# Loads of v on GpSimd's queue, new transfer times in the planner, copies of q by ScalarE or VectorE, and a tail matmul over 128 rows

## The chip, the core and the metric

The kernel runs on one core of a Trainium2 chip. The time is device microseconds of one execution. The kernel before was timed in 3 runs: median 733.4 us (730.46 to 735.7).

## What is computed

An attention layer with soft-capped scores, and behind it a feed-forward block without gating. Shapes: 4 batches, 12 heads, 448 positions, 64 values per head; 1792 tokens, model width 768, inner width 2048.

```python
def _attn_ref(q, k, v, cap):                       # 4, 12, 448, 64
    scores = 1.0 / np.sqrt(q.shape[-1]) * np.matmul(q, k.transpose(0, 1, 3, 2))
    scores = cap * np.tanh(scores / cap)
    scores = scores - np.max(scores, axis=-1, keepdims=True)
    attn = np.exp(scores)
    attn = attn / (np.sum(attn, axis=-1, keepdims=True) + 1e-09)
    return np.matmul(attn, v)

def _moe_ref(x, w_in, w_out):                      # 1792x768, 768x2048, 2048x768
    h = x @ w_in
    return (h - np.tanh(h)) @ w_out
```

The weights come as 64-bit floats and are turned into 32-bit ones on the core.

## The kernel before, in words

**Work.** Heads are taken in pairs (batch b, pair p; 24 pairs, 6 to a batch). For each pair q and k are loaded (`fetch_qk`), transposed by VectorE, and split into a high and a low part (`prep_pair`); v is loaded (`fetch_v`). Scores are matmuls over 448 columns on TensorE (line 689, one pass with the high part of q and one with the low part, so a block of scores is two matmuls), ScalarE makes tanh (line 699) and exp (line 757), and the product with v (PV) is accumulated on TensorE. The first 11 pairs (`F32_PAIRS`) make PV in plain 32-bit floats (`pv_f32`, line 825; 8 matmuls to a pair, each in two records of the trace). The other 13 pairs split v and exp into high and low parts (`pv`): per head 3 blocks of keys with three matmuls each (lines 852, 853, 854), and a tail block of 64 keys with two (lines 849 and 850). In the tail block the 64 keys stand twice on the 128 partitions, the high part of exp on one half and the low part on the other. Line 849 multiplies the low part of v with the high part of exp alone, so it takes 64 of the 128 rows.

**Feed-forward.** For each batch 16 blocks of inner width are worked through: `first` (lines 1159 to 1161) makes h, then tanh and a difference, and `second` (line 1212) accumulates the output. In batch 0's turn each block of weights is loaded (`fetch_raw`, lines 1000 and 1012, 1.5 MB a block), decoded by three passes of VectorE (lines 1042, 1049, 1056), split, and the decoded form is stored to memory by GpSimd's queue (line 986, tile fuk); later batches load it from there. The attention of batch b+1 is interleaved with the feed-forward of batch b.

**Order.** Nothing is ordered by hand. `Plan` collects all instructions with a cost, an engine, what they depend on, and the buffers they take, and then plays them through with these costs (`schedule`): each engine (TensorE, ScalarE, VectorE, SyncE's queue, GpSimd's queue) takes the instruction that can start first. A transfer costs its queue an issue time, and then stands in one line with all other transfers for `nbytes * slow / 360` ns. What comes out is a fixed order on each engine. So a changed cost reorders every engine.

**What the change touches.** `Build.dma` (line 441) holds the issue costs. `fetch_qk` and `fetch_v` issue on SyncE's queue (lines 473, 500, 502, 505). In `prep_pair`, the first 12 pairs need the high part of q on both halves of the partitions: for pair 0 of batch 0 and for the pairs of batch 1 ScalarE or VectorE copies it (`self.copy`, lines 422 and 424 in the trace), for the other 5 pairs of batch 0 a DMA of GpSimd's queue does (line 606). The buffers of v for the first 11 pairs are two (tag `v1`), so the load of pair i waits until PV of pair i-2 is done. The two buffers `vraw` serve the other pairs.

## Time and profile before

| | |
|---|---|
| median of 3 runs | 733.4 us |
| the profiled execution | 728.99 us, span 727.1 us |
| TensorE matmul busy | 700.3 us, 96% |
| ScalarE, VectorE busy | 530.4 us (73%), 508.0 us (70%) |
| GpSimd busy | 46.2 us (6%) |
| granted TensorE clock, mean | 0.994 of full speed |

The span is the time between the first and the last instruction of the profiled execution. PE is TensorE's matmul, DVE VectorE, ACT ScalarE, POOL GpSimd; SPq is SyncE's queue of DMAs. Matmuls are pipelined, so one record is longer than its share of the time: the distance from one start to the next is what a matmul takes. An idle time of an engine stands with what ended it.

### The profile page before, as it was taken

The numbers are of one execution on the slowest core, as the hardware profiler recorded it, in microseconds if no ns is written. First come the engines' busy times: TensorE is split into PE (matmuls) and PEld (weight loads), VectorE is DVE, ScalarE is ACT, GpSimd is POOL, SyncE is SP. The second block draws the span as 40 slices with busy tenths as digits, with TensorE's granted clock in tenths as the row PEclk, the third lists the DMA queues.
The fourth block names the chain that finished last, engine by engine and source line by source line (L and its number), as shares of the span: only waits on it lengthen the run. The fifth ranks groups of instructions, "written<-read, shape, count | busy, mean of one in ns | idle before, by whom it ended". The sixth has DMA issues, their size and how long they took to land.

```text
span 727.1 us, 10148 instructions
## 1 busy us (share of the span) xinstructions
PE 700.3 (96%) x3648; PEld 606.2 (83%) x3648; DVE 508.0 (70%) x775; ACT 530.4 (73%) x891; POOL 46.2 (6%) x93
## 2 busy tenths in 40 slices
PE   7989899999999999999999999999999999999996
PEld 5656687787788888889989897888989999999995
DVE  5889999997999986586678785786675333333331
ACT  7978957666677986677779898988896554545543
POOL 3110000000210110110110110110000000000000
PEclk9999999999999999999999999999999999999998
DMA  7999999999998593753765887777648656665523
GB/s 111 170 175 235 205 264 272 241 275 256 239 273 224 172 244 116 169 148 119 166 147 162 259 219 191 182 197 211 188 125 266 169 147 174 174 173 141 149 60 114
DMA packets 161823, 136.75 MB, mean 188 GB/s; under 512 B 116772, under 2 KB 146756, under 8 KB 161764
## 3 DMA queue, kind: packets, MB, share of 16 engines
q1 hardware_dynamic: 156676, 116.78, 66.7%
q0 software_dynamic: 5088, 19.24, 8.8%
q8 instruction: 31, 0.51, 0.3%
q14 instruction: 28, 0.23, 0.1%
HBM read 107.12 MB, written 18.09 MB: 172 GB/s over the span
## 4 chain that ended last, share of the span: by engine, by line
PE 54%; DVE 18%; DMA 14%; ACT 6%; issue 3%; SPq 3%; POOL 0%; DVEq 0%; ACTq 0%; POOLq 0%
PE facc L1212 18%; PE fh L1159 7%; PE fh L1161 7%; PE fh L1160 7%; DMA fw<-in_moe_w_in_dram 5%; PE fs L689 4%; DVE fu L1056 2%; DMA fkst<-fkst 2%; DVE fu L1049 2%; DMA fkst<-fkT 2%; DVE fwo L433 2%; PE fp L1212 2%; PE fs L1212 2%; PE fp L852 2%; DVE fu L1042 1%
## 5 line engine op out<-in xcount | busy, mean ns | idle before, releaser
L1212 PE MATMUL facc<-fwo,fgh 128*128 128x512 f32 (+1 forms) x768 | 171.4, 345 | 0.0
L1212 PEld LDWEIGHTS facc<-fwo,fgh 128*128 128x128 f32 x768 | 127.0, 188 | 20.1 <-issue 6.2
L1159 PE MATMUL fh<-fxh,fwi 128*128 128x384 f32 x384 | 135.3, 352 | 1.5 <-DVE fg L1174 1.5
L1161 PE MATMUL fh<-fxh,fwi 128*128 128x384 f32 x384 | 130.0, 339 | 0.0
L1160 PE MATMUL fh<-fxl,fwi 128*128 128x384 f32 x384 | 128.6, 335 | 0.0
L1212 PE MATMUL facc<-fwo,fgl 128*128 128x512 f32 (+1 forms) x384 | 98.6, 338 | 0.0
L433 DVE TENSOR_TENSOR fwi<-fu,fwi 128x768 fp32r<-128x768 f32 x66 | 62.9, 953 | 47.0 <-ACT fwi L422 46.6
L422 ACT CAST fwi<-fu 128x768 fp32r<-128x768 f32 x60 | 50.1, 835 | 44.0 <-PE fh L1161 29.7
L1159 PEld LDWEIGHTS fh<-fxh,fwi 128*128 128x128 f32 x384 | 72.1, 188 | 7.5 <-DVE fg L1174 2.9
L1160 PEld LDWEIGHTS fh<-fxl,fwi 128*128 128x128 f32 x384 | 72.2, 188 | 4.1 <-issue 2.6
L433 DVE TENSOR_TENSOR fwo<-fu,fwo 128x768 fp32r<-128x768 f32 x66 | 62.7, 950 | 15.7 <-ACT fwo L422 15.3
L1174 DVE TENSOR_TENSOR fg<-fh,fg 128x384 f32<-128x384 f32 x64 | 35.6, 556 | 53.5 <-ACT fg L1172 52.5
L1161 PEld LDWEIGHTS fh<-fxh,fwi 128*128 128x128 f32 x384 | 72.0, 187 | 0.0
L1212 PEld LDWEIGHTS facc<-fwo,fgl 128*128 128x128 f32 x384 | 58.8, 188 | 8.6
L699 ACT ACTIVATE fe<-fs 128x448 f32<-128x448 f32 x91 | 49.2, 541 | 18.9 <-PE fs L689 18.4
L689 PE MATMUL fs<-fqst,fkst 128*128 128x448 f32 x142 | 55.7, 412 | 3.9 <-ACT fe L699 2.0
L422 ACT CAST fwo<-fu 128x768 fp32r<-128x768 f32 x62 | 51.4, 829 | 8.8 <-PE facc L1212 8.3
L1172 ACT ACTIVATE fg<-fh 128x384 f32<-128x384 f32 x64 | 31.1, 485 | 34.4 <-PE fh L1161 34.3
L422 ACT CAST feh<-fe 128x896 fp32r<-128x896 f32 (+1 forms) x64 | 50.8, 793 | 0.8
L757 ACT ACTIVATE fe<-fe,absc 128x896 f32<-128x896 f32 (+1 forms) x52 | 49.6, 954 | 0.9
L433 DVE TENSOR_TENSOR fel<-fe,feh 128x896 fp32r<-128x896 f32 x39 | 42.2, 1081 | 10.4 <-ACT feh L422 10.3
L689 PE MATMUL fs<-fql,fkst 128*128 128x448 f32 x142 | 49.1, 366 | 0.0
(195 smaller groups left out, 1327.2 us busy)
## 6 DMA issues: line engine op xcount, KB each, us to landing
fu<-fuk SPq DMA_DIRECT2D x48, 768.0 KB
fw<-in_moe_w_in_dram SPq DMA_DIRECT2D x64, 384.0 KB
fw<-in_moe_w_out_dram SPq DMA_DIRECT2D x32, 768.0 KB
fuk<-fu POOLq DMA_DIRECT2D x16, 768.0 KB, 7.2
fqst<-fqh POOLq DMA_DIRECT2D x48, 112.0 KB, 5.5
fqraw<-in_q_dram SPq DMA_DIRECT2D x44, 112.0 KB
fkraw<-in_k_dram SPq DMA_DIRECT2D x44, 112.0 KB
out_dram<-fo SPq DMA_DIRECT2D x12, 384.0 KB
```

The lines of the kernel that those rows point to most:

```text
L422: self.nc.scalar.copy(out(), in_())
L433: lambda: self.nc.vector.tensor_sub(lo(), x(), hi().bitcast(F32)),
L689: nc.tensor.matmul(ps()[:, :S], self.keys(kst, h, c), q[:, h, :], start=n == 0, stop=n == passes - 1)
L699: S, lambda: nc.scalar.activation(dst(), ps()[:, :S], AF.Tanh), [o],
L757: lambda e=e, w=w: nc.scalar.activation(e()[:, :w, :], e()[:, :w, :], AF.Exp, scale=self.absc),
L852: nc.tensor.matmul(P()[:, :S], va, e, start=c == 0, stop=False)
L1159: nc.tensor.matmul(h()[:, :n], wh, ah, start=(d == 0), stop=False)
L1160: nc.tensor.matmul(h()[:, :n], wh, al, start=False, stop=False)
L1161: nc.tensor.matmul(h()[:, :n], wl, ah, start=False, stop=(d == ND - 1))
L1172: n, lambda: nc.scalar.activation(g()[:, :n], h()[:, :n], AF.Tanh), [prev], [g], [h], psum=True, key=k
L1174: o = self.dve(n, lambda: nc.vector.tensor_sub(g()[:, :n], h()[:, :n], g()[:, :n]), [o], [], [g, h], key=k + 600)
L1212: nc.tensor.matmul(banks[bk]()[:, c0 : c0 + ne], lhs()[:, ts], w()[:, k, e0 : e0 + ne], start=bk in firsts and bk not in begun, stop=stop ...
```

## The change

Five edits. The four loads of v of a pair are issued by GpSimd's queue in place of SyncE's. The copies of q in batch 0 are no DMAs any more: all are `self.copy`, and the planner chooses ScalarE or VectorE. The planner's costs change: issue of a DMA by SyncE 475 to 550 ns, by GpSimd 1016 to 600; the factor of q and k 2 to 2.3, of v 1 or 2 to 1.8, of the moves of k and q inside the chip 1 to 1.5. The tail's matmul with the low part of v takes all 128 rows, so the product of the two low parts is added, which the kernel before left out there. The new order follows from the costs.

```diff
     def dma(self, eng, nbytes, fn, deps=(), alloc=(), uses=(), slow=1, long=False, key=1e18):
-        c = (650.0 if long else 475.0) if eng == "SP" else 1016.0
+        c = (650.0 if long else 550.0) if eng == "SP" else 600.0
...
-                    self.dma("SP", np_ * S * 128, fn, [], [] if ops else [raw], [raw] if ops else [], slow=2)
+                    self.dma("SP", np_ * S * 128, fn, [], [] if ops else [raw], [raw] if ops else [], slow=2.3)
...
-                        nc.sync.dma_start(out=t[:, 0:3, :], in_=full.rearrange("(r c) d -> r c d", c=3))
+                        nc.gpsimd.dma_start(out=t[:, 0:3, :], in_=full.rearrange("(r c) d -> r c d", c=3))
                     elif f32:
-                        nc.sync.dma_start(out=t[TAIL * hp : TAIL * hp + TAIL, 3, :], in_=tail)
+                        nc.gpsimd.dma_start(out=t[TAIL * hp : TAIL * hp + TAIL, 3, :], in_=tail)
                     else:
-                        nc.sync.dma_start(out=t[:, 3, :], in_=tail.unsqueeze(0).to_broadcast([2, TAIL, D]))
+                        nc.gpsimd.dma_start(out=t[:, 3, :], in_=tail.unsqueeze(0).to_broadcast([2, TAIL, D]))
...
-                        "SP", (128 if part else FULL) * 256, fn, [], [] if ops else [vr],
-                        [vr] if ops else [], slow=1 + (f32 or part), long=f32 or part,
+                        "PL", (128 if part else FULL) * 256, fn, [], [] if ops else [vr],
+                        [vr] if ops else [], slow=1.8, long=True,
...
-                    [], [], [kst, T["k"]],
+                    [], [], [kst, T["k"]], slow=1.5,
...
-                if p == 0 or b:
-                    o3 = self.copy(
-                        S, lambda other=other, hp=hp: qst()[other, hp, :],
-                        lambda rows=rows, hp=hp: qst()[rows, hp, :].bitcast(F32), [o1], [], [qst],
-                    )
-                else:
-                    o3 = self.dma("PL", 64 * S * 4, dup, [o1], [], [qst])
+                o3 = self.copy(
+                    S, lambda other=other, hp=hp: qst()[other, hp, :],
+                    lambda rows=rows, hp=hp: qst()[rows, hp, :].bitcast(F32), [o1], [], [qst],
+                )
...
-                o3 = self.dma("PL", 64 * S * 4, dup, [o1], [] if i else [qst], [qh] + [qst] * (i > 0))
+                o3 = self.dma("PL", 64 * S * 4, dup, [o1], [] if i else [qst], [qh] + [qst] * (i > 0), slow=1.5)
...
                 if c == 3:
-                    nc.tensor.matmul(num, v2()[rows, c, hp, :], e[rows], start=False, stop=False)
+                    nc.tensor.matmul(num, v2()[:, c, hp, :], e, start=False, stop=False)
                     nc.tensor.matmul(P()[:, :S], va, e, start=False, stop=True)
```

How the order moves, at the places that the prediction speaks of. The first is SyncE's queue in batch 0, from the loads of k and q of pairs 2 and 3 on, before (fqraw and fkraw are q and k as loaded, fv1float the buffers of v of the first 11 pairs, fw a block of raw weights):

```order
L473 DMA fkraw_263<-in_k_dram 32x28x32 x4
L473 DMA fqraw_289<-in_q_dram 32x28x32 x4
L473 DMA fkraw_308<-in_k_dram 32x28x32 x2
L500 DMA fv1float_172<-in_v_dram 128x3x64 x2
L502 DMA fv1float_172<-in_v_dram 64x64 x2
L473 DMA fkraw_308<-in_k_dram 32x28x32 x2
L1000 DMA fw_50_356<-in_moe_w_in_dram 64x6x128 x2
L1012 DMA fw_50_356<-in_moe_w_out_dram 128x768
L473 DMA fqraw_382<-in_q_dram 32x28x32 x4
L473 DMA fkraw_408<-in_k_dram 32x28x32
L500 DMA fv1float_239<-in_v_dram 128x3x64 x2
L502 DMA fv1float_239<-in_v_dram 64x64 x2
```

And the same place in the changed kernel:

```order
L473 DMA fkraw_239<-in_k_dram 32x28x32 x4
L473 DMA fqraw_264<-in_q_dram 32x28x32 x4
L473 DMA fkraw_300<-in_k_dram 32x28x32 x4
L993 DMA fw_42_328<-in_moe_w_in_dram 64x6x128 x2
L1005 DMA fw_42_328<-in_moe_w_out_dram 128x768
L993 DMA fw_47_353<-in_moe_w_in_dram 64x6x128 x2
L1005 DMA fw_47_353<-in_moe_w_out_dram 128x768
L473 DMA fqraw_394<-in_q_dram 32x28x32 x4
```

The loads of v are gone from the queue, so 33 DMAs stand ahead of the first weights in place of 45, and the second block of weights follows the first at once.

The second place is GpSimd's queue in the changed kernel, from the load of v of pair 2 on (L979 is line 986 of before, the store of a decoded block of weights):

```order
L500 DMA fv1float_131<-in_v_dram 128x3x64 x2
L502 DMA fv1float_131<-in_v_dram 64x64 x2
L500 DMA fv1float_166<-in_v_dram 128x3x64 x2
L502 DMA fv1float_166<-in_v_dram 64x64 x2
L500 DMA fv1float_131<-in_v_dram 128x3x64 x2
L502 DMA fv1float_131<-in_v_dram 64x64 x2
L979 DMA fuk_87<-fu_486 128x1536
L500 DMA fv1float_166<-in_v_dram 128x3x64 x2
L502 DMA fv1float_166<-in_v_dram 64x64 x2
L500 DMA fv1float_131<-in_v_dram 128x3x64 x2
L502 DMA fv1float_131<-in_v_dram 64x64 x2
L979 DMA fuk_88<-fu_631 128x1536
```

The rows are the loads of pairs 2, 3, 4, a store, those of pairs 5 and 6, and a store. The loads of pairs 7, 8, 9 and 10 stand behind stores in the same way, and the loads of two late pairs (tile fvraw) stand just ahead of this place. In the kernel before this queue held the ten DMAs of q and the stores.

The third place is VectorE in batch 0, around the first decode in the changed kernel (fu is the block being decoded, fsumT_512 the sums of pair 2, fkst_103 and fql_107 the split k and q of pair 4):

```order
L909 TENSOR_TENSOR fx_475<-fnum_389,frb_458 128x384
L915 TENSOR_TENSOR fxt_116<-fnum_389,frb_458 128x64
L530 STREAM_TRANSPOSE fkT_482<-fkraw_300 128x448
L1035 TENSOR_SCALAR fu_486<-fw_42_328 128x1536
L424 CAST fkst_103<-fkT_482 64x448
L424 CAST fxh_495<-fx_475 128x384
L556 TENSOR_TENSOR fkst_103<-fkT_482,fkst_103 64x448
L424 CAST fkst_103<-fkT_482 64x448
L1042 SCALAR_TENSOR_TENSOR fu_486<-fw_42_328,fu_486 128x1536
L875 STREAM_TRANSPOSE fsumT_512<-fp_477 64x448
```

The first pass of the first decode (L1035, before L1042) stands ahead of the split of pair 4's k and of the sums of pair 2. Before, it stood behind the sums of pair 2 and the split of pair 4's k.

Over the whole program the copies of q on ScalarE go from 13 to 19 and on VectorE from 1 to 5; the count of matmuls stays the same.

## Rows read from the trace of the kernel before

**Rows 1.** Part 1 of the page: busy time, share of the span and count, by engine.

```profile
PE 700.3 (96%) x3648; PEld 606.2 (83%) x3648; DVE 508.0 (70%) x775; ACT 530.4 (73%) x891; POOL 46.2 (6%) x93
```

**Rows 2.** The view of stretches, all of the span: length, busy time and count of PE, PEld, DVE, ACT and POOL, granted clock, busy share of the DMA engines, GB/s.

```profile
0.00:20.00 20.00, 16.22 (x55) 11.97 (x55) 11.94 (x26) 14.92 (x25) 5.48 (x18) 1.00 0.75 113
20.00:40.00 20.00, 19.70 (x68) 13.30 (x66) 18.31 (x36) 18.61 (x32) 3.21 (x6) 1.00 1.21 186
40.00:60.00 20.00, 16.81 (x52) 11.15 (x53) 16.81 (x28) 15.92 (x28) 1.62 (x3) 0.91 1.03 182
60.00:140.00 80.00, 75.71 (x340) 59.97 (x339) 77.59 (x108) 58.32 (x98) 3.65 (x6) 1.00 1.04 242
140.00:226.00 86.00, 83.27 (x406) 69.42 (x405) 81.00 (x101) 61.12 (x100) 10.83 (x18) 1.00 1.07 259
226.00:540.00 314.00, 308.66 (x1617) 272.45 (x1616) 232.38 (x358) 261.04 (x421) 21.05 (x41) 1.00 0.68 181
```

**Rows 3.** The view of waits on PE from 0 to 226 us: who waited for whom, us in total, times, longest.

```profile
PE fp L825 <- DMA fv1float<-in_v_dram: 5.7, 3, 3.1
PE fp L825 <- DVE fsumT L882: 2.5, 3, 1.4
...
PE fs L689 <- DMA fqst<-fqst: 0.4, 1, 0.4
```

**Rows 4.** The timeline of PE around a tail block of PV at 229 us: start, us, line, tiles, shape (contraction rows * output rows, then the moving operand).

```profile
228.42 0.52 PE L1212 MATMUL facc<-fwo,fgh 128*128 128x512 f32 x2
228.77 0.51 PE L1212 MATMUL facc<-fwo,fgl 128*128 128x512 f32 x2
229.21 0.41 PE L849 MATMUL fp<-feh,fv 64*64 64x448 f32 x1
229.55 0.47 PE L850 MATMUL fp<-feh,fv1float32r 128*128 128x448 f32 x1
229.86 0.86 PE L1212 MATMUL facc<-fwo,fgh 128*128 128x512 f32 x4
```

**Rows 5.** The same around the last tail block, at 538 us, with two matmuls of the block ahead of it.

```profile
538.11 0.37 PE L853 MATMUL fp<-feh,fv 128*64 128x448 f32 x1
538.32 0.37 PE L854 MATMUL fp<-fel,fv1float32r 128*128 128x448 f32 x1
538.61 0.41 PE L849 MATMUL fp<-feh,fv 64*64 64x448 f32 x1
538.96 0.47 PE L850 MATMUL fp<-feh,fv1float32r 128*128 128x448 f32 x1
```

**Rows 6.** The instructions of lines 849 and 853: count, duration ns (least, median, most), first and last start, shape.

```profile
L849 PE MATMUL fp<-feh,fv x26: 410/415/418, 217.2 to 538.6; 64*64 64x448 f32 x26
...
L853 PE MATMUL fp<-feh,fv x78: 358/364/374, 209.3 to 538.1; 128*64 128x448 f32 x78
```

**Rows 7.** The timeline of SyncE's queue from 29.6 to 45.3 us: start and us of issue.

```profile
29.63 1.31 SPq L1000 DMA_DIRECT2D fw<-in_moe_w_in_dram  x2
30.98 0.67 SPq L1012 DMA_DIRECT2D fw<-in_moe_w_out_dram  x1
31.75 8.69 SPq L473 DMA_DIRECT2D fqraw<-in_q_dram  x4
...
41.48 2.47 SPq L500 DMA_DIRECT2D fv1float<-in_v_dram  x2
44.01 1.25 SPq L502 DMA_DIRECT2D fv1float<-in_v_dram  x2
```

**Rows 8.** The timeline of PE from 33.6 and from 41.4 us, across the longest wait for v.

```profile
33.61 1.67 PE L825 MATMUL fp<-fel,fv1float 128*128 128x448 f32 x4
35.11 0.92 PE L825 MATMUL fh<-fel,fv1float 128*128 128x448 f32 x2
...
41.41 0.37 PE L689 MATMUL facc<-fql,fkst 128*128 128x448 f32 x1
...
41.82 0.37 PE L689 MATMUL facc<-fql,fkst 128*128 128x448 f32 x1
45.27 2.35 PE L825 MATMUL fp<-feh,fv1float 128*128 128x448 f32 x4 [3.08 <-DMA fv1float<-in_v_dram]
```

**Rows 9.** The view of stretches, the stretch just behind that wait (columns as in rows 2).

```profile
46.30:49.60 3.30, 3.30 (x5) 1.35 (x4) 3.21 (x5) 0.39 (x1) 0.52 (x1) 0.50 0.97 158
```

**Rows 10.** GpSimd's DMAs of line 606, by form: count, busy us, mean ns of one issue, idle time before; and for line 606, and then for line 986, the time from issue to landing.

```profile
L606 POOL DMA_DIRECT2D fqst<-fqst x10 | 5.6, 562 | 42.4 <-ACT fqst L596 42.4
...
DMA to landing us min/median/max: 2.8/4.2/8.1
...
DMA to landing us min/median/max: 5.2/7.2/9.1
```

**Rows 11.** The copies of q from one half of the partitions to the other, by form: on ACT in the first 60 us, on DVE over the span (count, busy us, mean ns, idle before).

```profile
L422 ACT CAST fqst<-fqst 64x448 fp32r<-64x448 f32 x2 | 1.1, 565 | 0.1
...
L424 DVE CAST fqst<-fqst 64x448 fp32r<-64x448 f32 x1 | 0.4, 389 | 0.0
```

**Rows 12.** The timeline of DVE at the first pass of the first decode, and the waits of GpSimd for the decode and of DVE for the weights (us in total, times, longest).

```profile
43.52 0.96 DVE L1042 TENSOR_SCALAR fu<-fw 128x1536 uint32<-128x1536 uint32 x1
...
POOL fuk L986 <- DVE fu L1056: 145.8, 16, 17.5
...
DVE fu L1042 <- DMA fw<-in_moe_w_in_dram: 4.7, 3, 1.7
```

More of the change, by code (lines that the diff above doesn't have):

```diff
@@ L602, in lo @@
                     )
-                def dup(rows=rows, other=other, hp=hp):
-                    t = qst().bitcast(F32)
-                    nc.gpsimd.dma_start(out=t[other, hp, :], in_=t[rows, hp, :])
                 o1 = self.act(S, hi, [tr["q"][hp]], [] if hp else [qst], [T["q"]] + [qst] * hp, aps=1)
                 o2 = self.dve(S, lo, [o1], [] if hp else [ql], [qst, T["q"]] + [ql] * hp, extra=60)
-                if p == 0 or b:
-                    o3 = self.copy(
-                        S, lambda other=other, hp=hp: qst()[other, hp, :],
-                        lambda rows=rows, hp=hp: qst()[rows, hp, :].bitcast(F32), [o1], [], [qst],
-                    )
-                else:
-                    o3 = self.dma("PL", 64 * S * 4, dup, [o1], [], [qst])
+                o3 = self.copy(
+                    S, lambda other=other, hp=hp: qst()[other, hp, :],
+                    lambda rows=rows, hp=hp: qst()[rows, hp, :].bitcast(F32), [o1], [], [qst],
+                )
                 qops[hp] = [o1, o2, o3]
@@ L840, in pv @@
         P = self.plan.buf("h" if b == 0 and hp else "p")
-        rows = slice(D * hp, D * hp + D)
         prev = None
```

## The prediction, made before the changed kernel ran

> **What bounds the kernel now.** I read part 1 of the page first: TensorE's matmuls are busy 96% of the span [rows 1]. Where the other 4% lie is told by the view of stretches [rows 2]: TensorE idles 7.3 us in the first 60 us, 7.0 us from 60 to 226 us (4.29 and 2.73), 5.3 us from 226 to 540 us. The stages differ. From 60 to 226 us VectorE, which decodes the weights there, is nearly as full as TensorE (77.59 of 80 and 81.00 of 86 us); from 226 to 540 us TensorE alone is full (308.66 of 314), and what is cut from its work there is cut from the time. The view of waits [rows 3] says what ends its idle time up to 226 us: most of all the loads of v, 5.7 us in three waits. Last I read single matmuls [rows 4, 5]: a busy TensorE is not at its peak, and the distance from start to start shows where.
>
> **The tail matmul over 128 rows.** Line 849 is the only matmul of 64 by 64. Around it the distances are longer. Two matmuls of line 1212 (512 and 256 columns) take 0.35 us from 228.42 to 228.77; the two ahead of line 849 take 0.44 us, to 229.21: 0.09 lost before it. From line 849 to line 850 pass 0.34 us, from 850 to the next 0.31 us [rows 4], where 448 columns take 0.21 us from line 853 to 854 [rows 5]: 0.13 and 0.10 us lost. Together 0.32 us. The last of the 26 shows 0.29, 0.35 [rows 5] at the first two of these places, 0.08 and 0.14 over. The distances are read to 0.01 us, so it is 0.31 to 0.34 us each; for 26 of them [rows 6] 8.1 to 8.8 us. In the changed kernel the matmul has the shape of line 853, 128 rows by 64, and line 854 starts 0.21 us behind that [rows 5]: no loss. So I take -8.5 us. All 26 lie between 217 and 539 us [rows 6], where TensorE is the bound; nothing hides it.
>
> The Trainium skill, page "TensorEngine Tiling (Array Packing)", section "Tiling Modes", says that a change of tiling mode drains TensorE, and lists 128 by 64 as a mode of its own. Line 849's distances agree with it. By its wording line 853 would pay as well and this edit would bring nothing; line 853's distances say otherwise. The whole sum below would be -3 us by the rule and is -11.5 by the row.
>
> **The loads of v.** At 29.63 us SyncE issues 1.5 MB of weights, then four loads of q occupy it for 8.69 us, and only at 41.48 us does it come to the v of pair 3 [rows 7]. TensorE has nothing else from 41.82 us on and starts at 45.27 us, 3.08 us idle [rows 8]; behind that the granted clock is 0.50 for 3.3 us [rows 9], the lower of its two levels (1.2 instead of 2.4 GHz), which costs half of it, 1.7 us. The other two waits make up the 5.7 us. In the changed kernel these loads stand on GpSimd's queue, behind the wait for their buffer and, from pair 5 on, behind stores of decoded weights. What they need: four issues of 0.56 us as line 606 has them, or 0.62 to 1.24 us as SyncE had them for v, so 2.2 to 3.7 us [rows 7, 10], then 2.8 to 9.1 us to landing, as other DMAs of this queue took [rows 10]: 5.0 to 12.8 us, some 7 by the medians. What they have: counted in the new order between the last PV of pair i-2 and the first of pair i, at 0.41 us for a block of scores (two matmuls, 41.41 to 41.82) and 0.75 us for a matmul of line 825 (33.61 to 35.11 for two) [rows 8], TensorE's work is 13.0, 13.8, 10.1, 12.2 and 10.1 us for pairs 2 to 6 (before 9.7, 10.5, 10.5, 10.5, 9.7). So most or all of the waits go: up to -5.7, -1.7 with the clock, and -0.4 for the one wait for a DMA of q [rows 3], -7.8 in all. What is late next is VectorE: TensorE comes earlier to work that waits for decoded weights, for sums (2.5 us of its waits already end on fsumT [rows 3]) and for split k. VectorE has only 2.4 us idle from 60 to 140 us [rows 2]. The decode can start earlier, since 12 DMAs fewer stand ahead of the first weights (12 at about 0.6 us, some 7 us), and that gives it some of the lead back. I take half, -4 us, between 0 and -7.8.
>
> **The copies of q.** Ten DMAs become six casts on ScalarE and four on VectorE: 6 x 0.565 + 4 x 0.389 = 4.9 us [rows 11]. Both engines have cover in the first 60 us: ScalarE is busy 49.5 us and VectorE 47.1 [rows 2]. From 20 to 40 us only 1.4 and 1.7 us are idle, and about half of the casts fall there. Cost 0 to 4.9 us; I take +1.
>
> **The new order otherwise.** New costs shift every engine. TensorE's waits that the edits do not touch come to about 5 us up to 226 us and 5.3 us behind; a new order can halve them or add as much again. 0 us, between -5 and +5. The two late pairs' v loaded early, on DMA engines that are busy over 1.00 from 20 to 40 us [rows 2], belong here.
>
> **The sum.** -8.5 - 4 + 1 = -11.5 us, so the profiled execution of 728.99 us would become 717.5. That execution was 4.4 us under the median of the runs, 733.4; from the median the sum gives 721.9 us, which is my forecast.
>
> **Rivals.**
> - *Only the tail matmul counts.* VectorE holds the stretch to 226 us, and TensorE merely waits there for something else. For it: VectorE at 97% and 94% [rows 2]. Against: decoding can start earlier. 733.4 - 8.5 = 724.9 us.
> - *All of it counts,* waits, clock, and some of the other waits too: -8.5 - 7.8 - 2 = -18.3, so 715.1 us.
> - *VectorE is stuck on the first decode.* Its first pass now stands ahead of pair 4's split k and pair 2's sums. Before, it ran at 43.52 us with no wait [rows 12]; now its turn comes at about 34 us (an estimate from the work ahead of it, all of pair 1's and none of pair 2's PV), when the weights may still be on the way: DMA engines are full (1.21), and q and k of six pairs go first. If they land at 40 us, VectorE stands for 6 us, then TensorE, with a stretch at half clock (2 us) behind it: +8, which cancels the tail. 733 us, no difference. The other way round, DVE's waits for weights were 4.7 us in all and 1.7 at most [rows 12].
> - *GpSimd's queue holds v back: slower.* The loads of pairs 5, 7, 8, 9 and 10 now stand behind stores that wait for the decode, up to 17.5 us each [rows 12]. If each of the five came late as the worst one did before, 3.08 us and 1.7 at half clock, it is 24 us: 733.4 - 8.5 + 24 = 748.9 us. It decides from 3.2 us for each on (15.8 us, which uses up the 8.5 and 1% more). Against: in the new order the decode passes that these stores wait for stand ahead of the sums of the pair whose buffer is awaited, or shortly behind, and for pairs 8 to 10 TensorE has over 27 us of work in between.
> - *The drain goes with any change of shape.* Then 128 rows by 64 loses as much: no tail gain, 733.4 - 3 = 730.4 us. The Trainium skill's rule above is this rival's; line 853 speaks against it [rows 5].
>
> **Chances.** Forecast (718 to 724.5) 0.48; only the tail 0.22; all 0.10; stuck decode 0.12; held v 0.05; drain 0.03. The range from 713 to 729 us takes in the first three, 0.80. About 1% is what a measurement of this kernel can tell from no change: 726.1 us and below is faster, above 740.7 slower. Faster: 0.48 + 0.17 of the second + 0.10 = 0.75. Within 1%: 0.05 of the second, 0.11 of the third mechanism, 0.03: 0.19. Slower: 0.06.
>
> **What the changed profile would show.** Line 842 (849 before) with shape 128*64, 0.21 us from its start to the next and from there to the one behind; TensorE's busy time lower by some 8 us with the same count of matmuls. No wait of L825's successor (L818) for v over 1 us, and no stretch at clock 0.50 before 100 us. Waits on DVE (sums, kst) in the place of part of them; ScalarE's and VectorE's busy time in the first 60 us up by some 5 us. If the idle time of TensorE from 0 to 226 us is above 14.3 us, as it was, the middle term was wrong; if 128*64 keeps the long distances, the first; if TensorE waits for v with GpSimd idle on a store ahead of it, the queue rival is right.

## The result, and the profile after

The changed kernel was slower: median 739.1 us (737.3 to 742.4, 4 runs) against 731.9 (729.4 to 735.7, 4 runs) of the kernel before beside it, ratio 1.0108 (95% interval 1.0065 to 1.0151). The forecast was 721.9 us, and 739 lies outside its range of 713 to 729 us. The profiled execution took 737.32 us, span 735.5 us. Line numbers behind the edit of `prep_pair` are 7 lower than before (849 is 842, 689 is 682, 638 is 631, 1070 is 1063).

Part 1 of the page, as in [rows 1]:

```profile
PE 700.1 (95%) x3648; PEld 611.3 (83%) x3648; DVE 510.9 (69%) x781; ACT 532.9 (72%) x895; POOL 111.9 (15%) x179
```

GpSimd went from 46.2 to 111.9 us: the issues of v. The stretches of [rows 2], now:

```profile
0.00:20.00 20.00, 16.62 (x59) 13.20 (x60) 12.96 (x28) 15.41 (x26) 16.80 (x33) 1.00 1.03 128
20.00:40.00 20.00, 15.33 (x49) 10.24 (x48) 13.90 (x29) 15.42 (x26) 4.43 (x7) 0.91 1.21 175
40.00:60.00 20.00, 19.68 (x62) 12.04 (x62) 19.52 (x35) 19.05 (x33) 5.17 (x7) 1.00 1.11 202
60.00:140.00 80.00, 75.55 (x333) 58.75 (x332) 78.81 (x110) 61.03 (x103) 15.91 (x25) 1.00 0.99 227
140.00:226.00 86.00, 82.82 (x394) 69.26 (x393) 78.64 (x101) 60.04 (x98) 18.69 (x30) 0.98 1.06 244
226.00:540.00 314.00, 301.54 (x1595) 272.18 (x1594) 230.85 (x349) 252.79 (x411) 50.53 (x77) 0.99 0.71 181
```

TensorE idles 16.0 us up to 226 us (14.3 before), and 12.5 us from 226 to 540 us (5.3 before). The second number is the news: that stage was taken for full. Up to 700 us there are also three stretches at the lower clock, where before had one [rows 9]. The view of stretches for these (columns as in rows 2):

```profile
29.66:33.07 3.41, 3.41 (x7) 1.76 (x6) 3.28 (x7) 2.08 (x4) 0.00 (x0) 0.50 1.07 151
152.54:155.95 3.41, 3.41 (x12) 3.41 (x11) 3.35 (x4) 1.95 (x3) 1.32 (x2) 0.50 0.24 32
528.00:534.83 6.83, 5.41 (x16) 4.57 (x16) 5.24 (x9) 6.70 (x12) 0.00 (x0) 0.50 0.27 98
```

They add up to 13.7 us, and TensorE is busy for 12.2 of them. At this clock the same matmuls took 1.8 times as long (the 18 matmuls measured under 7 and 8), so an estimate of what is lost is 5.4 us, against 1.5 before. That makes up for about half of the 8 us by which the tail should have lowered TensorE's busy time; why the rest of it did not show is not accounted for.

The tail itself did what was forecast. The timeline of PE around one tail block, which answers to [rows 4]:

```profile
232.91 0.52 PE L1205 MATMUL facc<-fwo,fgh 128*128 128x512 f32 x2
233.26 0.51 PE L1205 MATMUL facc<-fwo,fgl 128*128 128x512 f32 x2
233.60 0.37 PE L842 MATMUL fp<-feh,fv 128*64 128x448 f32 x1
233.81 0.36 PE L843 MATMUL fp<-feh,fv1float32r 128*128 128x448 f32 x1
234.01 0.86 PE L1205 MATMUL facc<-fwo,fgh 128*128 128x512 f32 x4
```

From 842 to 843 pass 0.21 us and 0.20 to the next, where [rows 4] had 0.34 and 0.31; ahead of 842 pass 0.34, which is what the two matmuls there need (0.35 from 232.91 on). The instructions of line 842, as in [rows 6], are all of this shape:

```profile
L842 PE MATMUL fp<-feh,fv x26: 361/366/374, 220.8 to 547.4; 128*64 128x448 f32 x26
```

The waits of PE over the span, which answer to [rows 3]:

```profile
PE fs L682 <- ACT fe L692: 9.6, 9, 2.4
PE fs L682 <- ACT feh L692: 5.0, 3, 2.6
PE facc L682 <- DVE fkst L556: 4.5, 2, 3.7
```

No wait for v is left. TensorE waits for tanh (line 692) and for the split k. The longest, 3.7 us, is in batch 0. The timeline there, of VectorE, GpSimd and PE:

```profile
25.56 0.65 DVE L530 STREAM_TRANSPOSE fkT<-fkraw 128x448 f32<-128x448 f32 x1 [6.32 <-DMA fkraw<-in_k_dram]
...
10.49 1.55 POOL L500 DMA_DIRECT2D fvraw<-in_v_dram  x2
12.04 1.67 POOL L505 DMA_DIRECT2D fvraw<-in_v_dram  x2
13.70 1.54 POOL L500 DMA_DIRECT2D fvraw<-in_v_dram  x2
15.23 1.78 POOL L505 DMA_DIRECT2D fvraw<-in_v_dram  x2
...
28.87 0.54 PE L682 MATMUL facc<-fqst,fkst 128*128 128x448 f32 x1 [3.75 <-DVE fkst L556]
```

VectorE stands 6.3 us for k of a pair of batch 0, and in the time ahead of it GpSimd issues v of two late pairs (fvraw). That these loads are what delays k is not shown. The view of waits on ACT from 226 to 540 us has two rows that stand out:

```profile
ACT fqh L614 <- DMA fqst<-fqh: 16.6, 6, 6.0
...
ACT fw L1063 <- DMA fw<-in_moe_w_in_dram: 5.0, 1, 5.0
```

The first (3.3 us in two waits before) is for the four copies of q by DMA (line 631). They stand on GpSimd's queue, and there now is v. The kernel before has 48 such copies on this queue too, from 188 us on (line 638); the account of the queue ahead of the prediction names only the ten DMAs of q in batch 0 and the stores. The second is `inspect`, which reads each block of weights once more for a check of its range.

### The profile page after: what moved, and what is told of

The parts are those of the page before. It is cut to its first block, busy times and chain, and to the rows that moved or that the text cites. A ratio compares the mean times of both kernels' runs of the same rounds, so it can differ in the third digit from the quotient of the medians.

```text
span 735.5 us, 10142 instructions
## 1 busy us (share of the span) xinstructions
PE 700.1 (95%) x3648; PEld 611.3 (83%) x3648; DVE 510.9 (69%) x781; ACT 532.9 (72%) x895; POOL 111.9 (15%) x179
## 4 chain that ended last, share of the span: by engine, by line
PE 41%; DVE 22%; DMA 18%; ACT 8%; issue 4%; SPq 3%; POOL 2%; DVEq 0%; ACTq 0%
PE facc L1205 14%; DMA fw<-in_moe_w_in_dram 9%; PE fh L1152 6%; PE fh L1154 6%; PE fh L1153 6%; DMA fqst<-fqh 3%; DVE fu L1042 2%; DVE fu L1049 2%; PE fs L682 2%; DVE fsumT L875 2%; DVE fwo L433 2%; DMA fkraw<-in_k_dram 2%; DMA fkst<-fkT 2%; PE fp L1205 2%; PE fs L1205 2%
## 5 line engine op out<-in xcount | busy, mean ns | idle before, releaser
L1152 PE MATMUL fh<-fxh,fwi 128*128 128x384 f32 x384 | 137.4, 358 | 1.4 <-DVE fg L1167 1.4
L1154 PE MATMUL fh<-fxh,fwi 128*128 128x384 f32 x384 | 131.2, 342 | 0.0
L1152 PEld LDWEIGHTS fh<-fxh,fwi 128*128 128x128 f32 x384 | 72.9, 190 | 8.5 <-DVE fg L1167 3.4
L422 ACT CAST fwi<-fu 128x768 fp32r<-128x768 f32 x57 | 47.6, 835 | 40.4 <-PE fh L1154 28.4
L1154 PEld LDWEIGHTS fh<-fxh,fwi 128*128 128x128 f32 x384 | 73.0, 190 | 0.0
L433 DVE TENSOR_TENSOR fel<-fe,feh 128x896 fp32r<-128x896 f32 x39 | 42.2, 1082 | 16.6 <-ACT feh L422 16.2
L682 PEld LDWEIGHTS fs<-fqst,fkst 128*128 128x128 f32 x142 | 33.0, 237 | 24.7 <-ACT fe L692 13.4
L422 ACT CAST fgh<-fg 128x384 fp32r<-128x384 f32 x64 | 32.8, 512 | 24.7 <-DVE fg L1167 22.2
```

Source lines behind the costliest of these rows:

```text
L422: self.nc.scalar.copy(out(), in_())
L433: lambda: self.nc.vector.tensor_sub(lo(), x(), hi().bitcast(F32)),
L682: nc.tensor.matmul(ps()[:, :S], self.keys(kst, h, c), q[:, h, :], start=n == 0, stop=n == passes - 1)
L1152: nc.tensor.matmul(h()[:, :n], wh, ah, start=(d == 0), stop=False)
L1154: nc.tensor.matmul(h()[:, :n], wl, ah, start=False, stop=(d == ND - 1))
```

## The experiments

Two theories. **Queue:** loads of v on GpSimd's queue hold back what stands behind them. **Order:** the planner's new order puts engines behind late transfers, whatever the queue. Where a kernel keeps an order, only the issuing engine or a body is exchanged, and the planner's numbers stay those of that order. To match two kernels of one order matmul by matmul means to compare the start of the same matmul in both traces. All ratios are to the kernel before, timed beside. One kernel's runs spread over up to 17 us (before: 726 to 743 us in all), so an interval is about 0.7% wide, some 5 us, and a difference between two kernels of less than about 4 us is weak.

### 1. The tail alone

```diff
-                    nc.tensor.matmul(num, v2()[rows, c, hp, :], e[rows], start=False, stop=False)
+                    nc.tensor.matmul(num, v2()[:, c, hp, :], e, start=False, stop=False)
```

> The kernel before with the tail's matmul over 128 rows and nothing else; the order on every engine is that of before. Both theories (the loss comes from v on GpSimd's queue; the loss comes from the new order) expect the distances of the changed kernel, 0.33 us less at each of 26 places, so -8.7 us: 731.9 - 8.7 = 723.2 us, and TensorE's busy time at 692 us. If the time is above 727 us, the tail is worth less than its distances and part of the loss is not a loss.

Measured: 730.8 us, ratio 0.9966 (0.9928 to 1.0005). That is 0.34%, some 2.5 us in place of 8.7, with the order unchanged. The waits of PE from 200 to 560 us tell where the rest went, first before, then with the tail alone:

```profile
PE fs L689 <- ACT fe L699: 2.0, 3, 1.3
PE fh L1159 <- DVE fg L1174: 1.5, 1, 1.5
PE fp L852 <- ACT fnum L422: 1.3, 2, 1.1
PE fp L852 <- DVE fsumT L882: 0.9, 2, 0.5
```

```profile
PE fs L689 <- ACT fe L699: 5.7, 6, 1.7
PE fp L852 <- ACT fnum L422: 2.5, 2, 1.5
PE fh L1159 <- DVE fg L1174: 1.8, 1, 1.8
PE fp L852 <- DVE fsumT L882: 1.6, 4, 0.4
```

5.7 us of waits became 11.6 in these four rows: 5.9 us of the 8.7 were given back, and 8.7 - 5.9 = 2.8 us is the gain of the profiled spans (727.1 to 724.8) within half a us. Over the whole span TensorE is busy 6.3 us less and idle 4.0 us more.

### 2. and 3. The queue exchanged, the order kept

The second kernel is the tail alone, with v issued by GpSimd; the third is the changed kernel, with v issued by SyncE. The diff shows one of the three lines that change alike, in the second kernel; in the third they change the other way.

```diff
-                        nc.sync.dma_start(out=t[:, 0:3, :], in_=full.rearrange("(r c) d -> r c d", c=3))
+                        nc.gpsimd.dma_start(out=t[:, 0:3, :], in_=full.rearrange("(r c) d -> r c d", c=3))
...
```

> The kernel before with the 128-row tail, and the loads of v issued by GpSimd's queue at the places in the program where SyncE issued them; the order on TensorE, ScalarE and VectorE is that of before. Theory 'queue' (GpSimd's queue takes the loads of v early, so k lands late in batch 0, and the copies of q that stand behind v on this queue come late from 226 us on): the time is 6 to 12 us above the kernel with the tail alone, 729 to 735 us, with waits of ScalarE for fqst above 10 us in sum behind 226 us. Theory 'order' (the engines' new order stands behind late transfers, whatever the queue): within 3 us of the tail alone or up to 4 us faster, 719 to 726 us.

> The changed kernel with the loads of v issued by SyncE at the same places in the program; the order on TensorE, ScalarE and VectorE is that of the changed kernel. Theory 'queue': more than half of the 17 us of new losses go, 739 - 9 to 739 - 15, so 724 to 730 us, the waits of ScalarE for fqst behind 226 us fall from 16.6 us to about 3, the stall of ScalarE for fw at 520 us stays. Theory 'order': 735 to 743 us; v is late again in batch 0 besides, which may add some us.

Measured: 736.8 us, 1.0080 (1.0045 to 1.0116), above the tail alone by 6 us (medians) or 1.14% (ratios), with not one instruction of TensorE, ScalarE or VectorE moved: the 6 to 12 us that the queue theory gave (its 729 to 735 us were counted from a tail alone at 723.2). And 735.4 us, 1.0044 (1.0013 to 1.0075): some 4 us below the changed kernel, short of the queue theory. ScalarE's waits for the copies of q behind 226 us are 11.7 us there, where about 3 were expected. This run does not separate the two theories, since v stands between q and k on SyncE's queue again: in batch 0 TensorE waits 5.61 us for the split k at 23.27 us (3.75 in the changed kernel). Matched matmul by matmul, the third kernel is 6.5 us behind the changed kernel at 62 us and 0.9 ahead of it at the end.

### 4. Planned anew with v on SyncE

```diff
-                        "PL", (128 if part else FULL) * 256, fn, [], [] if ops else [vr],
+                        "SP", (128 if part else FULL) * 256, fn, [], [] if ops else [vr],
```

> The changed kernel with the loads of v given back to SyncE in the planner too (issue 650, factor 1.8, so it plans anew), with the other new costs, the copies of q and the tail kept. Theory 'queue': 722 to 729 us, since nothing stands behind v on GpSimd's queue. Theory 'order': the plan is another one again, and its time is anywhere between 720 and 742 us, with stalls at other places; a stall at a late reload of weights (fw, 4.95 us in the changed kernel) need not come back.

Measured: 729.8 us, 0.9967 (0.9937 to 0.9997). With the other new costs, the copies and the tail kept, giving v back takes 9 to 10 us off; the kernel is then as fast as the tail alone. ScalarE still waits 10.1 us for the copies of q from 200 to 560 us, with no v on their queue, so this wait by itself does not measure the loss.

### 5. and 6. Later passes of inspect, without and with the tail

Only the first pass of `inspect` carries the mark `lag`; the planner makes a new order from it.

```diff
-        return LAT
+        return LAT + (6000.0 if to.lag and o.dma else 0.0)
```

> The kernel before; in the planner alone the first pass of inspect counts its reloaded weights as landed 6 us later, so it stands later in ScalarE's order. Theory 'reloads' (with the tail alone ScalarE stood at two inspect passes behind reloads of 1.5 MB, 4.2 and 3.7 us, and TensorE behind it; that is where the tail's gain went): those waits go here too, 2.8 and 2.0 us in before, and the time is 2 to 4 us below before, 728 to 730 us. Rival 'everywhere' (a faster TensorE meets ScalarE and VectorE at many places; the reloads are two of them): 730 to 734 us.

> The same with the 128-row tail. Theory 'reloads': the tail now brings 7 us or more against the kernel with the lag alone, 721 to 724 us, and no wait of ScalarE for fw above 1 us. Rival 'everywhere': the tail brings 2 to 4 us again, 726 to 731 us, and TensorE's waits from 206 us on stay near 11 us, behind tanh and sums of other places.

Measured: 728.3 us, 0.9950 (0.9916 to 0.9985), and 725.4 us, 0.9922 (0.9885 to 0.9959). The lag alone brings 0.5%, and ScalarE's waits for the reloads are gone (3.3 us in two waits before, from 200 to 560 us); that the gain is theirs is likely but not shown, since the whole order is new. The tail brings 0.28% on top, no more than before. 'Reloads' falls as the account of the tail. 'Everywhere' has the tail's 2 to 4 us right; TensorE's waits from 206 us on are 8.3 us, less than its 11, and 3.9 without the tail.

### 7. and 8. The first pairs' v, the late pairs' v

The tail alone, order kept, with one half of the loads on GpSimd's queue. The diff shows one of three lines of the seventh kernel; in the eighth the two queues change places.

```diff
-                        nc.sync.dma_start(out=t[:, 0:3, :], in_=full.rearrange("(r c) d -> r c d", c=3))
+                        (nc.gpsimd if f32 else nc.sync).dma_start(out=t[:, 0:3, :], in_=full.rearrange("(r c) d -> r c d", c=3))
...
```

> The kernel before with the 128-row tail, in its own order; v of the first 11 pairs (plain 32-bit) is issued by GpSimd's queue, v of the other 13 by SyncE's. Of the 6 us that all loads of v on GpSimd's queue cost in this order, theory 'late pairs' (the copies of q stand behind loads of v from 226 us on) expects 0 to 2 here: 729 to 733 us, ScalarE's waits for fqst near 4 us. Theory 'batch 0 and 1' expects 4 to 6: 735 to 737 us, with the stall of sums at 114 us (3.8 us, then 6.8 us at half clock).

> The other half: v of the 13 late pairs on GpSimd's queue, v of the first 11 on SyncE's. Theory 'late pairs': 4 to 6 us above the tail alone, 735 to 737 us, ScalarE's waits for fqst above 9 us in sum. Theory 'batch 0 and 1': 0 to 2 us, 731 to 733 us.

Measured: 727.9 us, 0.9959 (0.9918 to 0.9999) for the first pairs, and 738.2 us, 1.0090 (1.0053 to 1.0126) for the late ones. The whole cost is the late pairs': 1.0090 against 0.9966 is 1.24%, 9.1 us (7.3 by the medians). One place shows how. GpSimd's, SyncE's, ScalarE's and PE's timelines at the first load of kept weights (fu<-fuk), with the tail alone:

```profile
214.61 2.08 POOL L638 DMA_DIRECT2D fqst<-fqh  x4 [7.83 <-PE fs L689]
217.64 0.56 POOL L986 DMA_DIRECT2D fuk<-fu  x1 [0.95 <-DVE fu L1056]
...
225.61 0.39 SPq L979 DMA_DIRECT2D fu<-fuk  x1
...
231.38 0.83 ACT L422 CAST fwi<-fu 128x768 fp32r<-128x768 f32 x1 [1.15 <-DMA fu<-fuk]
...
232.91 0.44 PE L852 MATMUL fp<-feh,fv1float32r 128*128 128x448 f32 x1 [1.02 <-ACT fnum L422]
...
236.32 0.36 PE L853 MATMUL fp<-feh,fv 128*64 128x448 f32 x1
```

And with late v on GpSimd's queue:

```profile
216.55 0.54 POOL L638 DMA_DIRECT2D fqst<-fqh  x1 [7.82 <-PE fs L689]
218.22 0.77 POOL L500 DMA_DIRECT2D fvraw<-in_v_dram  x1 [1.13 <-ACT fe L757]
218.98 0.53 POOL L638 DMA_DIRECT2D fqst<-fqh  x1
219.51 1.65 POOL L505 DMA_DIRECT2D fvraw<-in_v_dram  x2
...
221.68 0.81 POOL L500 DMA_DIRECT2D fvraw<-in_v_dram  x1
...
223.93 0.59 POOL L986 DMA_DIRECT2D fuk<-fu  x1
...
231.52 0.35 SPq L979 DMA_DIRECT2D fu<-fuk  x1
...
236.68 0.83 ACT L422 CAST fwi<-fu 128x768 fp32r<-128x768 f32 x1 [4.51 <-DMA fu<-fuk]
...
238.20 0.71 PE L852 MATMUL fp<-feh,fv1float32r 128*128 128x448 f32 x1 [4.37 <-ACT fnum L422]
...
244.34 0.37 PE L853 MATMUL fp<-feh,fv 128*64 128x448 f32 x1
```

The wait of SyncE there, and the stretch behind TensorE's stall (columns as in rows 2):

```profile
SPq L979 <- DMA fuk<-fu: 5.1, 1, 5.1
```

```profile
237.44:244.20 6.76, 6.00 (x18) 5.71 (x19) 4.61 (x8) 4.64 (x9) 0.00 (x0) 0.50 0.35 119
```

The four loads of v stand between the copies of q, and the store of a decoded block (L986) is behind all of them: issued at 223.93 in place of 217.64, 6.3 us later. Of these, 1.9 us are older than this place, since the first copy is as late; 4.4 arise here, where issuing v takes 3.2 us and its first load waits 1.1 us for the buffer. SyncE's load (L979) waits 5.1 us for that store and starts 5.9 us later; ScalarE, in order, stands 4.51 us in place of 1.15; TensorE stands 4.37 in place of 1.02, and then the granted clock is 0.50 for 6.8 us. The 18 matmuls from this L852 to the L853 shown behind it take 6.14 us in place of 3.41, 1.8 times as long. That is 3.35 + 2.73 = 6.1 us at one place. By the end the two profiled spans are 12.7 us apart: 1.9 us of this were there ahead of the place, and nearly all of the rest comes behind 440 us. Besides, ScalarE's waits from 200 to 560 us for the copies of q went from 3.9 to 10.2 us and for reloads from 6.7 to 9.8; the view of waits with late v on GpSimd's queue:

```profile
ACT fqh L621 <- DMA fqst<-fqh: 10.2, 3, 4.8
ACT fw L1070 <- DMA fw<-in_moe_w_in_dram: 9.8, 4, 4.4
```

Once issued, the copies land as fast as with the tail alone (5.1 us in the median in both), so it is their place in the queue that makes them late. But the two longest of these waits, 4.83 us at 283.83 and 3.28 us at 311.56, cost TensorE nothing: matched matmul by matmul, its lag is 8.0 us at the end of the place above and 7.1 us behind both.

### 9. The late pairs' v back on SyncE, in the changed kernel

```diff
-                        nc.gpsimd.dma_start(out=t[:, 0:3, :], in_=full.rearrange("(r c) d -> r c d", c=3))
+                        (nc.gpsimd if f32 else nc.sync).dma_start(out=t[:, 0:3, :], in_=full.rearrange("(r c) d -> r c d", c=3))
...
```

> The changed kernel in its own order; v of the 13 late pairs is issued by SyncE again, v of the first 11 stays on GpSimd's queue. Theory 'late pairs' (late v on GpSimd's queue holds back the copies of q and the stores of decoded weights that stand behind it): 5 to 9 us below the changed kernel, 730 to 734 us, ScalarE's waits for fqst behind 226 us at 4 us in place of 16.6. Theory 'order' (the changed kernel's order is bad by itself): 736 to 740 us. The stall of ScalarE for fw at 520 us stays by both.

Measured: 729.8 us, 0.9984 (0.9950 to 1.0018), 1.24% below the changed kernel: the same 9.1 us in another order. ScalarE's wait for the copies of q is down to this row (7.5 in place of 16.6 us, more than the 4 expected):

```profile
ACT fqh L614 <- DMA fqst<-fqh: 7.5, 5, 4.1
```

TensorE's waits from 200 to 560 us fall from 13.2 to 7.0 us, its time at half clock there from 6.8 to 3.4. The places are not those of kernel 8. Matched matmul by matmul, kernel 9 gains nothing at the store and is 9.0 us ahead at the end; the largest steps are 0.9 us at 309 us, 2.1 at 447 and 1.7 at 526, each at a wait of TensorE for tanh. VectorE's wait for k in batch 0 stays (5.9 us in place of 8.0): which queue issues late v does not decide it.

### 10. GpSimd held without loads

In place of the late loads of v (which stay on SyncE), GpSimd clears a small scratch tile three times; 1.08 us, a little longer than an issue.

```diff
+ [nc.gpsimd.memset(self.idle, 0.0) for _ in range(0 if f32 or self.general else 3)]
```

> The kernel before with the 128-row tail, all of v on SyncE; at each place where a load of v of the 13 late pairs is issued, GpSimd clears a scratch tile three times (about 0.9 us), so its queue is held about as long as by issuing that load (0.77 to 0.83 us), with no transfer and without the load's wait for its buffer. Theory 'held by issue': 3 to 7 us above the tail alone, 734 to 738 us. Rival 'buffer wait or transfer' (what holds the queue is the wait of the load for its buffer, or the bytes): 729 to 732 us.

Measured: 734.2 us, 1.0007 (0.9969 to 1.0045). By the median it is 3.3 us above the tail alone, but the intervals overlap. Its interval also lies below that of kernel 8, though GpSimd is held a little longer than by the loads' issue, which speaks against the issue time as the whole cost. TensorE's longest stall, 4.41 us at 238 us, is like that of kernel 8, but SyncE came late to its load by itself there (229.15 us, 225.61 with the tail alone). Inconclusive: how much of the 9.1 us is issue time, how much the load's wait for its buffer, and how much the bytes, stays open.

### 11. and 12. Both mends together

The eleventh has the edits of 1, 5 and 7 (the order is that of 6). The twelfth is the kernel of 4 with the edit of 5, planned anew.

> The kernel before with the 128-row tail, the 6 us of lag for the reloads in the planner, and v of the first 11 pairs on GpSimd's queue. If the waits for v in batch 0 (5.7 us before) can be had without the late pairs' cost: 722 to 726 us, that is up to 3 us below the tail with the lag. If VectorE's sums and decode take their place: 725 to 729 us.

> The changed kernel with v given back to SyncE in the planner (as in the run that was planned anew) and the 6 us of lag for the reloads. ScalarE waited there 8.5 us for reloads; if these are worth what they were in the order of before, 724 to 728 us; if other waits take their place, 729 to 731 us.

Measured: 724.2 us, 0.9893 (0.9855 to 0.9932), and 725.1 us, 0.9901 (0.9867 to 0.9935). Both are faster than before by about 1%. The first has the lowest median of this study; their intervals overlap, and that of kernel 6 too.

### 13. and 14. The old tail in two other kernels

The changed kernel, and kernel 11, with the matmul over 64 rows again; the orders stay.

```diff
-                    nc.tensor.matmul(num, v2()[:, c, hp, :], e, start=False, stop=False)
+                    nc.tensor.matmul(num, v2()[rows, c, hp, :], e[rows], start=False, stop=False)
```

> The changed kernel, same order, with the tail's matmul over 64 rows as before. If the tail is worth 8.5 us where TensorE does not wait: 747 us. Theory 'given back' (TensorE waits for ScalarE and VectorE at fixed places of the order, and what it gains ahead of them it loses there): 2 to 4 us above the changed kernel, 741 to 743 us, ratio to before 1.013 to 1.017.

> The fastest kernel so far (lag for the reloads, first v on GpSimd's queue), same order, with the tail's matmul over 64 rows. Tail worth 8.5 us: 733 us. Theory 'given back': 726 to 729 us.

Measured: 743.4 us, 1.0155 (1.0115 to 1.0195), and 728.8 us, 0.9950 (0.9916 to 0.9984). The tail is worth 0.47% and 0.57% there, 3.4 and 4.2 us, about as 'given back' expected, and half of 8.5 at best.

### 15. and 16. Without the passes of inspect

The range check of the weights is left out; its reloads stay. The diff shows the first of the two passes, and the second goes the same way.

```diff
-            n, lambda: nc.scalar.activation(x(), x(), AF.Abs, accum_out=self.seen[:, 0, f : f + 1]),
+            n, lambda: None,
...
```

> The kernel before without ScalarE's two inspect passes over each reloaded block of weights (the range check of the weights is left out; the reloads themselves stay), order otherwise as before. ScalarE has some 54 us less to do behind 380 us and waits for no reload. Before shows only 1.8 us of TensorE waits behind 380 us, so by both theories 1 to 3 us below before: 728 to 731 us.

> The same without the passes, with the 128-row tail. Theory 'ScalarE's passes and reloads take the gain back' (the tail alone showed 6.0 us of TensorE waits behind 380 us, before 1.8): the tail brings 6 to 8 us here, 721 to 724 us. Rival 'everywhere': 2 to 4 us, 726 to 728 us, with TensorE's waits behind 200 us near 9 us.

Measured: 727.6 us, 0.9942 (0.9916 to 0.9969), and 724.7 us, 0.9905 (0.9872 to 0.9938): the tail brings 0.37%, 2.7 us, again. ScalarE's passes do not take the gain back; the theory fell. What does is seen at 442 to 448 us. The timelines of DVE and PE without the tail, and with it:

```profile
445.64 0.65 DVE L530 STREAM_TRANSPOSE fkT<-fkraw 128x448 f32<-128x448 f32 x1 [3.69 <-DMA fkst<-fkT]
...
448.33 0.47 PE L852 MATMUL fp<-feh,fv1float32r 128*128 128x448 f32 x1 [1.57 <-DVE fsumT L882]
```

```profile
443.26 0.65 DVE L530 STREAM_TRANSPOSE fkT<-fkraw 128x448 f32<-128x448 f32 x1 [5.22 <-DMA fkst<-fkT]
...
445.95 0.47 PE L852 MATMUL fp<-feh,fv1float32r 128*128 128x448 f32 x1 [3.44 <-DVE fsumT L882]
```

By start less idle time, TensorE comes there at 446.76 (448.33 - 1.57) and, with the tail, at 442.51 (445.95 - 3.44): 4.25 us earlier. VectorE, which has to take that pair's sums behind this transpose, starts it only 2.4 us earlier, since it waits for a move of k inside the chip (fkst<-fkT). The chain of work shows two such moves one behind the other there, 8.67 and 2.62 us without the tail, 9.98 and 2.66 us with it: they did not shrink. So TensorE waits 1.9 us longer, and behind this wait the granted clock is 0.51 in the mean from 447.1 to 450.5 us, close to its lower level, where it is 1.00 without the tail. Matched matmul by matmul, the lead of 4.25 us is 0.8 us from 451 us on.

### 17. and 18. The change mended, and the copies alone

The seventeenth is the changed kernel with the edit of 9, late v on SyncE in the planner too (the first diff), and the edit of 5. The eighteenth is the tail alone, with the ten DMAs of q in batch 0 as copies, order kept (the second diff).

```diff
-                        "PL", (128 if part else FULL) * 256, fn, [], [] if ops else [vr],
+                        "PL" if f32 else "SP", (128 if part else FULL) * 256, fn, [], [] if ops else [vr],
```

```diff
-                    nc.gpsimd.dma_start(out=t[other, hp, :], in_=t[rows, hp, :])
+                    nc.scalar.copy(*t) if hp or p % 5 == 0 else nc.vector.tensor_copy(*t)
```

> The changed kernel with v of the 13 late pairs on SyncE in the planner and in fact, v of the first 11 on GpSimd's queue, and the 6 us of lag for the reloads; planned anew. Theory 'late pairs': no stall behind late v is left, 722 to 728 us, as the two other kernels with the lag and without late v on GpSimd's queue (724.2 and 725.1). If the order of the changed kernel in batch 0 (k late behind early loads) comes back in the plan, 728 to 732 us.

> The kernel before with the 128-row tail, order kept; the ten DMAs that copy q in batch 0 are six copies by ScalarE and four by VectorE at the same places. The forecast's term was +1 us (0 to 4.9) against the tail alone, 730.8 us: 731 to 736 us. If the copies fill idle time and the wait for the DMA of q (0.4 us before) goes: 729 to 731 us.

Measured: 728.6 us, 0.9939 (0.9912 to 0.9965), at the border of its two cases; by the medians it is slower than kernels 11 and 12, though the intervals overlap. Its trace has another loss in place of late v: up to 200 us TensorE waits 10.6 us for sums (fsumT), 0.7 in the changed kernel, and up to 80 us the clock is 0.50 for 13.7 us. And 727.1 us, 0.9935 (0.9906 to 0.9963), 0.31% below the tail alone: no cost of the copies is seen, and they may gain 2 us.

## Why the prediction was wrong

**The tail, -8.5: the mechanism right, the term mis-sized.** The trace shows the distances that were forecast, so the rival of the drain is out. The Trainium skill, page "TensorEngine Tiling (Array Packing)", section "Tiling Modes", says that every change of mode drains TensorE and lists 128 by 64 as a mode. Here 128 rows by 64 among 128 by 128 stand 0.20 to 0.21 us apart, and the measurement decides. The step that failed is "All 26 lie between 217 and 539 us, where TensorE is the bound; nothing hides it." Five pairs of kernels, each of one order, give 0.34, 0.28, 0.37, 0.57 and 0.47%, 0.4% in the mean or 3 us; alone, four of the five are within noise. They cover three orders, that of before, that of the lag and that of the changed kernel. A busy share of 98% was read as a bound of one engine; but ScalarE and VectorE wait there for transfers whose times do not shrink with TensorE, and TensorE meets them at fixed places of the order: in the tail alone its waits from 200 to 560 us grew by 5.9 us, and in the other four pairs by 2.9 to 5.7. Shown are the waits; that transfers are the root of each of them is shown at the place of experiment 16 alone.

**The loads of v, -4: the wrong loads were priced.** The term spoke of pairs 2 to 10. For those it had the right sign: no wait for v is left in the changed kernel, and their loads on GpSimd's queue measure -0.07% (7 against 1) and -0.29% (11 against 6), 0.5 to 2 us, none of it certain. The stretch at the lower clock was priced at half its length, 1.7 us; by the 18 matmuls of kernel 8 it costs 1.5. Left out were the 13 late pairs, whose v moved as well. What the loads are moved past was counted for SyncE's queue, and for v behind stores; not counted were the stores and copies of q that now stand behind v. That is +9.1 us, twice, in both orders. That late v on GpSimd's queue costs this is shown by kernels 8 and 9; the way to TensorE was followed at one place, the store that accounts for 6.1 us of kernel 8's profile, and for the rest it is open.

**The rivals.** The queue rival had the right queue and the wrong direction: it had v late behind stores (none was), where stores and copies of q were late behind v. The stuck decode did not come: VectorE's longest wait for weights up to 226 us was 3.3 us. By its own tests the prediction is refuted at the middle term: TensorE's idle time up to 226 us is 16.0 us, above 14.3. Three more signs failed: TensorE's busy time fell by 0.2 us in place of 8, a stretch at clock 0.50 came before 100 us (at 29.66), and in the first 60 us ScalarE and VectorE were busy 49.9 and 46.4 us (49.5 and 47.1 before), not 5 us more.

**The copies, +1.** They last as priced, 6 x 0.557 + 4 x 0.387 = 4.9 us in kernel 18, and no cost of it is seen: 0 to -2 us.

**The new order, 0.** With all but late v the changed kernel stands at 0.9984; the tail, the first pairs' v and the copies alone would make 0.9966 x 0.9993 x 0.9969 = 0.9928. The difference, 0.56% or 4 us, is put down to the new order, within the -5 to +5 given, though the intervals leave it uncertain by as much. k late in batch 0 may be part of it. The sum of the measured terms: -2.5 - 0.5 - 2.3 + 4.1 + 9.1 = 7.9 us, and measured were 1.08% of 731.9, 7.9 us; it closes because the order's term is the remainder.

## What to carry to other kernels

When a transfer is moved to another queue, list what stands behind it there at every stage of the program, not only where the gain is looked for, and follow the latest of these to the engine that waits. When work is cut on an engine that is 98% busy, ask where it will next wait for an engine that follows a transfer: here the waits grew by about half of the cut, and the time fell by a third of it. Change a queue and an order in separate kernels; a planner fed with new costs does both at once.

## What was not expected of the hardware

A late store cost nearly as much by the clock as by the wait: it made TensorE's wait 3.35 us longer, and behind it, at a granted clock of 0.50 for 6.8 us, 18 matmuls took 2.73 us longer. They took 1.8 times as long at half the clock, not twice. By the granted clock of its profile kernel 8 spent 23.9 us at the lower level up to 700 us (the tail alone 3.4). Issuing one load of v takes GpSimd 0.77 to 0.84 us in the median (lines 500 and 505 in kernel 8), where a copy of q takes 0.52, so a pair's four loads hold this queue for 3.2 us.
